# Attention pairs turned by transposing transfers, and the order of the first three pairs

## The chip, the cores and the metric

The kernel runs on one core of a Trainium2 chip. The metric is the device time of one execution in microseconds (us). Five engines work side by side, each through its own list of instructions in order: TensorE (PE, its weight loads PEld), VectorE (DVE), ScalarE (ACT), GpSimd (POOL) and SyncE (SP). SP and ACT also issue transfers (DMA); an instruction that waits holds up everything behind it on its engine.

## What the reference computes

```python
q_n, k_n, c_n = (t / (norm(t, axis=-1) + 1e-6) for t in (q, k, centroids))   # q, k, v: (4, 8, 768, 64)
q_assign = argmax(einsum('bhsd,hcd->bhsc', q_n, c_n), -1)                     # 16 centroids per head
k_assign = argmax(einsum('bhsd,hcd->bhsc', k_n, c_n), -1)
mask = q_assign[:, :, :, None] == k_assign[:, :, None, :]
scores = where(mask, q @ k.T / sqrt(64), -1e9)
x = softmax(scores) @ v            # (4, 8, 768, 64) -> x: (3072, 512)
h = maximum(x @ w_in, 0)           # w_in: 512 x 2048
out = (h * h) @ w_out              # w_out: 2048 x 512
```

A token attends only to tokens of its own cluster, and the result feeds a two-layer network with a squared ReLU.

## The kernel before, in words

The attention goes over 16 pairs of heads (`for p in range(NG)`), the rest of the time is the network. Each engine's order is the order of the program text (a manual schedule), so what stands earlier in the text is issued earlier on that engine.

For each pair the kernel needs `qkT[pair]`, q and k with the head dimension on the partitions, and marks that say which cluster a token belongs to.

- Pair 0 is turned by matmuls against an identity (`turn_first`, L280, copied at L285); pair 1 too, in three parts (`turn`, L295, copied at L299). From pair 2 on, `split_words` copies q and k as 16-bit halves on ACT (L315), stores them to DRAM (`words`, L316), and `turn_words` reads them back with one transposing transfer on SP (L327).
- `logits` (L335) multiplies with the centroids into a bank "ls". `turn_logits` (L346) turns it on DVE and `number` finds the first of the largest logits (L357 to L362). For pair 0 the result is a one-hot tile `oh`, turned by PE in `turn_onehot` (L402). For the other pairs `number` writes small marks (to L379), which go to DRAM and back as `rows`: `far` (L383), then two `rows` transfers (L386) that wait for `far`, all on SP.
- A tile of scores is a mask (L456) and a product (L447) added in a PSUM tile "sc" (`tile_of`), then an exponential on ACT (L463). Nine tiles make a pair. There are three "sc" buffers, used in turn by `begin`: the bank "ls", with the next logits and the sums of `add_up` (L500), takes one of the three as well.
- DVE adds the exponentials up (L466). PE multiplies with v (`times_v`, L481, banks V and M). `add_up` sums over partitions, `invert` (L509, L513) takes reciprocals and stores them (`far_r`, L515), `spread` reads them back into `rb` for all partitions (two transfers, L522), and `finish` (L545) scales a pair's result with `rb`. `finish(p - 1)` stands behind pair p's additions on DVE, followed by `round_2` (L151 to L159) on a block of w_in. At the top of pair p + 1 come `invert(p)`, `turn_logits` and `number` of pair p + 2.
- `load_qk`, `load_v` and `load_ahead` (blocks of weights, L128) issue loads on SP, except that from pair 4 on q and k go through ACT's queue.

Pools: six buffers for q and k ("qk", also used by `flat`), nine for exponentials ("ex"), three `qkT`.

Of the kernel before, what the change touches and what calls it, by code (L numbers as in the profile page):

```python
# [8 lines left out]
F32 = mybir.dt.float32  # L9
# [9 lines left out]
P = 128  # L19
# [6 lines left out]
def kernel(  # L26
# [196 lines left out]

    seen = const.tile([P, NG * NBL], F32, name="seen")

    oh = accp.tile([P, NBL, 2, D], BF16, name="oh", tag="part")
# [10 lines left out]
    def centroids_norm():  # L237
        sq = once.tile([P, D], F32, name="cen_sq")
        ss = const.tile([P, 1], F32, name="cen_ss")
        nc.vector.tensor_tensor(out=sq, in0=cen, in1=cen, op=ALU.mult)  # L240
        nc.vector.reduce_sum(out=ss, in_=sq, axis=AX.X)
        nc.vector.tensor_scalar_max(out=ss, in0=ss, scalar1=1e-30)
        nrm = const.tile([P, 1], F32, name="cen_nrm")
        nc.scalar.sqrt(nrm, ss)
        warm = once.tile([P, 1], F32, name="warm")
        nc.scalar.activation(out=warm, in_=ss, func=ACT.Exp, scale=0.0)
        for _ in range(2):
            r = small.tile([P, 1], F32, name="cen_r")
            nc.vector.reciprocal(out=r, in_=nrm)
            twice = small.tile([P, 1], F32, name="cen_twice")  # L250
            nc.vector.scalar_tensor_tensor(
                out=twice, in0=ss, scalar=r, in1=nrm, op0=ALU.mult, op1=ALU.add
            )
            nc.vector.tensor_scalar_mul(out=nrm, in0=twice, scalar1=0.5)
        nc.vector.tensor_scalar_add(out=nrm, in0=nrm, scalar1=1e-6)
        rden = const.tile([P, 1], F32, name="cen_rden")
        nc.vector.reciprocal(out=rden, in_=nrm)
        for e in range(2):
            nc.vector.tensor_scalar(
                out=cn[:, e], in0=cen, scalar1=rden, scalar2=odd[:, e : e + 1],  # L260
                op0=ALU.mult, op1=ALU.mult,
            )
# [25 lines left out]

    def turn(pair, part, bank):
        if part == 0:  # L290
            qkT[pair] = qktp.tile([P, 2 * NCH, P], F32, name="qkT")
        for i in range(4):
            which, c = divmod(4 * part + i, NCH)
            for e in range(2):
                nc.tensor.matmul(  # L295
                    bank[D * e : D * (e + 1), P * i : P * (i + 1)],
                    lhsT=raw[pair][which][:, e, c], rhs=ident, start=True, stop=True,
                )
        nc.scalar.copy(  # L299
            out=qkT[pair][:, 4 * part : 4 * part + 4].rearrange("p c n -> p (c n)"), in_=bank  # L300
        )
        if part == 2:
            raw.pop(pair)

    words = {}

    def split_words(pair, which, queue=nc.sync):
        if pair >= NG:
            return
        if which == 0:  # L310
            words[pair] = dram.tile([2 * NCH, P, 2, 2 * D], U16, name="words")
        flat = loads.tile([P, NCH, 2, 2 * D], U16, name="flat", tag="qk")
        src = raw[pair][which].bitcast(U16).rearrange("p h c (d two) -> p h c two d", two=2)
# [9 lines left out]
    def turn_words(pair):  # L323
        if pair >= NG:
            return
        qkT[pair] = qktp.tile([P, 2 * NCH, P], F32, name="qkT")
        nc.sync.dma_start(  # L327
            qkT[pair].rearrange("p c n -> p (c n)").bitcast(U16),
            words.pop(pair).rearrange("c p two d -> (c p two) d"), transpose=True,
        )  # L330

# [16 lines left out]
    def number(pair):  # L348
# [7 lines left out]

        nc.vector.reduce_max(out=mx, in_=src, axis=AX.X)  # L357
        nc.vector.tensor_tensor(out=best, in0=src, in1=over_c(mx), op=ALU.is_ge)
        nc.vector.tensor_tensor(
            out=best, in0=best, in1=order.unsqueeze(1).to_broadcast([P, n, C]), op=ALU.mult  # L360
        )
        nc.vector.reduce_max(out=mx, in_=best, axis=AX.X)  # L362
        if pair == 0:
            nc.vector.tensor_tensor(
                out=oh.rearrange("p b e c -> p (b e) c")[:, :, 0:C], in0=best, in1=over_c(mx),
                op=ALU.is_equal,
            )
            return
        squared = small.tile([P, n], F32, name="squared")
# [15 lines left out]
        for e in range(2):  # L385
# [3 lines left out]
            )  # L389

    def turn_onehot():
        spare = expp.tile([P, 2, 512], F32, name="ex").bitcast(BF16)
# [3 lines left out]

        for half, bank in enumerate((sc.pop("oh")[:, 0], M)):
            n = NBL // 2
# [204 lines left out]
    def load_ahead(rounded):  # L603
        nonlocal loaded
        while loaded < min(rounded + (6 if stage_2 else 3), N_IN + FT):
            load_weights(loaded)
            loaded += 1

    centroids_norm()
    turn_first(0, 0, V, nc.scalar.copy)  # L610
# [3 lines left out]
    centroids_turned()  # L614
    turn_first(1, 1, halves[1], nc.vector.tensor_copy)
    logits(0, begin("ls"))
    for i in ("oh", 0, 1):
        begin(i)
    turn_logits(0)
    number(0)  # L620

    first_sums = []
# [7 lines left out]
    for p in range(NG):  # L630
        if p == 0:
            load_qk(3)
            load_ahead(0)
        if p == HP + 1:
            nc.sync.dma_start(x_far[FEED[3]], xT.pop(FEED[3]))
        if p:
            invert(p - 1)
            if p == NG - 1:
                early_x_sums()
            turn_words(p + 2)  # L640
            spread(p - 1)
        if 2 < p + 1 < NG:
            turn_logits(p + 1)
            number(p + 1)
        load_v(p + 1)
        if p:
            load_ahead(p - 1)


        if p == 0:  # L650
            for i in range(2):
                turn(1, i, (V, M)[i])
                score(p, i, 0, True)
            turn_onehot()
            for t in rows_of:
                nc.vector.memset(t, 0.0)
            turn(1, 2, V)
            for i in range(NB):
                if i == 2:
                    begin(i)  # L660
                    score(p, i, 0, True)
                mask(p, i, 0, False)
                exponential(i)
        else:
            for i in range(NB):
                tile_of(p, i)
        total[p] = endp.tile([P, 2, S], F32, name="total")
        first, last = total[p][:, :, 0:QA], total[p][:, :, QA:S]
        add(nc.vector, first, ex[0], ex[1])
        if p == 1:  # L670
            tile_of(p, NB)
        if p < 2:
            logits(p + 1, begin("ls"))
            turn_logits(p + 1)
            number(p + 1)
        add(nc.vector, first, first, ex[2])
        for i in range(NB, NCH):
            if p != 1 or i > NB:
                tile_of(p, i)
            add(nc.vector, first, first, ex[i])  # L680
        if p == 0:
            for i in range(2):
                split_words(2, i, nc.scalar)
            turn_words(2)
        else:
            split_words(p + 3, 0)


        for i in range(NCH, NCH + NB):
            tile_of(p, i)  # L690
        part = accp.tile([P, 2, 512], F32, name="part")
        add(nc.vector, part, ex[NCH], ex[NCH + 1])
# [1011 lines left out]
    def fine_sums():  # L1704
        nc.vector.scalar_tensor_tensor(
            out=seen, in0=seen, scalar=2.0 ** -100, in1=seen, op0=ALU.is_ge, op1=ALU.is_gt,
            accum_out=fine,
        )

    def check_sums():  # L1710
        every = more.tile([1, 1], F32, name="every", tag="more")
        nc.tensor.matmul(every, lhsT=fine, rhs=ups[:, 0:1], start=True, stop=True)
        nc.vector.tensor_scalar(
            out=flag[0:1], in0=every, scalar1=UP * float(P * NG * NBL), scalar2=None, op0=ALU.is_lt
        )
# [279 lines left out]
```

## Time and profile before

| | us |
|---|---|
| median of 3 runs (lowest, highest) | 861.9 (861.75, 864.93) |
| the profiled execution's own time | 864.17 |
| its span, first to last instruction | 862.3 |
| PE busy in the span | 854.2 |
| DVE busy | 740.9 |
| ACT busy | 452.6 |
| POOL busy | 246.6 |

The span is what the views of the trace divide up; the profiled execution's own time is 1.87 us longer. The attention takes roughly the first 320 us of it, some 19 us for each pair once it runs evenly. The first three pairs, the ones that the change touches, lie before 75 us.

### The profile page before, as it was taken

To read this page: it belongs to the slowest core of one execution; us is meant where nothing else is said; L and a number is where in the kernel's file an instruction comes from. 1 tells how busy PE (TensorE), PEld (TensorE's weight loads), DVE (VectorE), ACT (ScalarE), POOL (GpSimd) and SP (SyncE) were. 2 spreads that over 40 slices of the span, in tenths; PEclk is the share of its full clock that TensorE was granted. 3 is DMA by queue.
4 is the path that set the end of the run, shared out by engine and by line. 5 is a ranking of instruction groups with operands and counts; after the bars stand their busy time and mean duration, and the time that the engine had idled before them with its cause. 6 is when DMAs were issued, how large, how long until landed. Compare 5 with 4: busy or idle time off the path is not lost.

```text
span 862.3 us, 15571 instructions
## 1 busy us (share of the span) xinstructions
PE 854.2 (99%) x5883; PEld 648.9 (75%) x5883; DVE 740.9 (86%) x1192; ACT 452.6 (52%) x697; POOL 246.6 (29%) x232
## 2 busy tenths in 40 slices
PE   9999999999999999999999999999999999999997
PEld 6444444444444445557899999999999999999997
DVE  5799888888888899899788988799888997888786
ACT  4877766677776557753212683222268322584120
POOL 0000001000000046772587537130223902337000
PEclk9999999999999999999999999999999999999999
DMA  7676797777766217829897744459447895434542
GB/s 258 156 199 178 202 285 202 192 184 197 196 173 179 67 44 240 259 73 322 326 334 279 235 159 156 175 165 338 145 183 234 289 364 200 181 137 137 219 153 72
DMA packets 149732, 174.36 MB, mean 202 GB/s; under 512 B 57258, under 2 KB 126994, under 8 KB 146322
## 3 DMA queue, kind: packets, MB, share of 16 engines
q1 hardware_dynamic: 133090, 152.94, 56.2%
q10 hardware_dynamic: 16560, 20.35, 7.2%
q8 instruction: 48, 0.79, 0.4%
q14 instruction: 34, 0.28, 0.1%
HBM read 111.98 MB, written 50.27 MB: 188 GB/s over the span
## 4 chain that ended last, share of the span: by engine, by line
PE 92%; DVE 4%; ACT 2%; issue 1%; DMA 0%; DVEq 0%
PE bank L1390 22%; PE bank L1113 17%; PE sc L447 14%; PE av_a L481 10%; PE bank L811 7%; PE bank L1287 6%; PE more L1113 5%; PE av_b L481 5%; PE sc L456 4%; PE sc L335 1%; PE sc L500 1%; DVE home L557 1%; ACT g L786 1%; ACT g L787 1%; DVE w_raw L155 1%
## 5 line engine op out<-in xcount | busy, mean ns | idle before, releaser
L463 ACT ACTIVATE ex<-sc 128x1024 f32<-128x1024 f32 x144 | 144.4, 1026 | 37.5 <-PE sc L447 31.6
L447 PE MATMUL sc<-qkT 64*128 64x512 f32 (+1 forms) x768 | 150.5, 484 | 0.0
L167 POOL TENSOR_TENSOR w_in<-w_in,w_raw 128x512 int32<-128x512 int32 x16 | 21.4, 1335 | 296.4 <-DVE w_in L159 296.4
L1098 POOL TENSOR_TENSOR g<-g,home 128x384 f32<-128x384 f32 x60 | 60.4, 1038 | 155.4 <-DVE home L1202 101.9
L447 PEld LDWEIGHTS sc<-qkT 64*128 64x128 f32 x768 | 65.7, 188 | 42.1 <-issue 30.2
L481 PE MATMUL av_a<-ex,v_raw 128*64 128x512 f32 x384 | 85.9, 596 | 0.0
L466 DVE TENSOR_TENSOR total<-total,ex 128x1024 f32<-128x1024 f32 x64 | 78.7, 1229 | 6.5
L1647 ACT COPY spare<-bank 128x128 f32<-128x128 f32 x35 | 9.2, 263 | 132.3 <-issue 69.7
L1390 PE MATMUL bank<-wt,l 128*128 128x128 f32 x544 | 72.0, 275 | 0.4 <-DVE l L557 0.4
L1390 PE MATMUL bank<-wt,home 128*128 128x128 f32 x552 | 70.5, 275 | 0.0
L1390 PEld LDWEIGHTS bank<-wt,l 128*128 128x128 f32 x544 | 66.2, 192 | 0.6 <-DVE l L557 0.6
L1390 PEld LDWEIGHTS bank<-wt,home 128*128 128x128 f32 x552 | 66.0, 192 | 0.0
L481 PEld LDWEIGHTS av_a<-ex,v_raw 128*64 128x64 f32 x384 | 26.2, 137 | 51.0 <-issue 50.3
L1202 DVE TENSOR_TENSOR g<-bank,g 128x384 f32<-128x384 f32 (+2 forms) x108 | 53.2, 505 | 10.7 <-PE bank L1113 6.6
L1080 ACT COPY home<-bank 128x384 f32<-128x384 f32 x66 | 30.9, 480 | 54.9 <-PE bank L1113 53.5
L456 PE MATMUL sc<-rows 64*128 64x512 bf16 (+1 forms) x360 | 58.8, 323 | 0.0
L786 ACT ACTIVATE g<-g 128x768 f32<-128x768 f32 (+1 forms) x77 | 54.8, 712 | 4.6 <-DVE g L1202 3.3
L787 ACT ACTIVATE g<-g 128x768 f32<-128x768 f32 (+1 forms) x77 | 55.7, 723 | 2.4
L481 PE MATMUL av_b<-ex,v_raw 128*64 128x256 f32 x384 | 44.2, 379 | 0.0
L481 PEld LDWEIGHTS av_b<-ex,v_raw 128*64 128x64 f32 x384 | 27.6, 137 | 20.7 <-issue 5.7
L456 PEld LDWEIGHTS <-rows 64*128 64x128 bf16 x360 | 17.5, 94 | 33.6 <-issue 30.4
L1390 PE MATMUL bank<-wt,g 128*128 128x128 f32 x304 | 39.1, 276 | 0.0
(296 smaller groups left out, 1857.4 us busy)
## 6 DMA issues: line engine op xcount, KB each, us to landing
wt<-right_far SPq DMA_DIRECT2D x11, 1792.0 KB
wt<-w_far SPq DMA_DIRECT2D x20, 896.0 KB
words<-flat SPq DMA_DIRECT2D x26, 384.0 KB
w_raw<-in_moe_w_in_dram SPq DMA_DIRECT2D x16, 512.0 KB
w_raw<-in_moe_w_out_dram SPq DMA_DIRECT2D x16, 512.0 KB
wt<-right_far SPq DMA_DIRECT2D x7, 1024.0 KB
v_raw<-in_v_dram SPq DMA_DIRECT2D x16, 384.0 KB
raw<-raw_far SPq DMA_DIRECT2D x12, 512.0 KB
```

Of the source, the lines that this page charges most:

```text
L447: nc.tensor.matmul(sc[i][:, e, cols], lhsT=qkT[pair][rows, NCH + c], rhs=qkT[pair][rows, n.start // P : n.stop // P], start=first, stop=no ...
L456: nc.tensor.matmul(sc[i][:, e, cols], lhsT=ohT[pair][rows, 1, c * P : (c + 1) * P], rhs=ohT[pair][rows, 0, columns(i)], start=first, stop= ...
L463: nc.scalar.activation(out=ex[i], in_=sc.pop(i), func=ACT.Exp, scale=SCALE)
L466: eng.tensor_tensor(out=out, in0=a, in1=b, op=ALU.add)
L481: nc.tensor.matmul(bank[D * e : D * (e + 1), 0 : n.stop - n.start], lhsT=raw_v[pair][:, e, c], rhs=ex[i][:, e, cols], start=c == 0, stop=c ...
L786: nc.scalar.activation(out=to, in_=to, func=ACT.Relu)
L787: nc.scalar.square(to, to)
L811: nc.tensor.matmul(bank, lhsT=operands[j][0][:, kk], rhs=operands[j][1][:, kk], start=(kk == 0), stop=(kk == H2 - 1),)
L1098: nc.gpsimd.tensor_tensor(out=of_four(to, s)[:, f, half], in0=of_four(base, s)[:, f, half], in1=beside[s][:, u], op=ALU.add,)
L1113: nc.tensor.matmul(bank[:, QT * u : QT * (u + 1)], lhsT=lefts[j, s](u)[i], rhs=operand[i], start=begins and u == 0, stop=True, skip_group_ ...
L1202: nc.vector.tensor_tensor(out=out, in0=one, in1=two, op=ALU.add)
L1390: nc.tensor.matmul(bank, lhsT=left[:, f], rhs=rhs[:, f], start=(f == 0), stop=(f == F4 - 1))
```

## The change

Pair 1 is no longer turned by PE. `split_words(1, ..)` runs on ACT before the loop, with its two `flat` tiles in "ex" buffers, and `turn_words(1)` issues two transposing transfers, one for q and one for k. On SP this stands ahead of `load_qk(3)` and of two blocks of weights (three before). The last copy of pair 0's k is shared by ACT and DVE (`by_two`).

Pair 0's marks are written straight from the comparison with the maximum; `count_marks` counts them into the tile `single`, and the check at the end takes it in.

Pair 0's third score now stands before the masks. `logits(1)`, its turning and numbering move from the fourth tile of pair 0 to behind its eighth, into bank M, followed by `turn_words(2)` and `load_v(1)` on SP. Pair 1 computes two scores before its first mask, which needs `rows`. `logits(2)` and `number(2)` move from behind its fourth tile to behind its sixth, and `spread(0)` and the third block of weights come behind `number(2)`; `load_v(2)` comes ahead of `turn_words(3)`.

```diff
@@ split_words / turn_words
-        flat = loads.tile([P, NCH, 2, 2 * D], U16, name="flat", tag="qk")
+        if pair == 1:
+            spare = expp.tile([P, 2, 512], F32, name="ex").bitcast(U16)
+            flat = spare.rearrange("p a n -> p (a n)")[:, 0 : 4 * S // 2].rearrange(
+                "p (c two d) -> p c two d", c=NCH, two=2
+            )
+        else:
+            flat = loads.tile([P, NCH, 2, 2 * D], U16, name="flat", tag="qk")
...
-        nc.sync.dma_start(
-            qkT[pair].rearrange("p c n -> p (c n)").bitcast(U16),
-            words.pop(pair).rearrange("c p two d -> (c p two) d"), transpose=True,
-        )
+        far = words.pop(pair)
+        for i in range(0, 2 * NCH, NCH if pair == 1 else 2 * NCH):
+            c = slice(i, i + (NCH if pair == 1 else 2 * NCH))
+            nc.sync.dma_start(
+                qkT[pair][:, c].rearrange("p c n -> p (c n)").bitcast(U16),
+                far[c].rearrange("c p two d -> (c p two) d"), transpose=True,
+            )
@@ number
+        if pair == 0:
+            nc.vector.tensor_tensor(
+                out=oh.rearrange("p b e c -> p (b e) c")[:, :, 0:C], in0=src, in1=over_c(mx),
+                op=ALU.is_ge,
+            )
+            return
...
-        if pair == 0:
-            nc.vector.tensor_tensor(
-                out=oh.rearrange("p b e c -> p (b e) c")[:, :, 0:C], in0=best, in1=over_c(mx),
-                op=ALU.is_equal,
-            )
-            return
@@ new functions
+    def count_marks():
+        marked = small.tile([P, 1], F32, name="marked")
+        nc.vector.reduce_sum(
+            out=marked, in_=oh.rearrange("p b e c -> p (b e) c")[:, :, 0:C], axis=AX.XY
+        )
+        nc.vector.tensor_scalar(
+            out=single, in0=marked, scalar1=2.0 * NBL, scalar2=None, op0=ALU.is_equal
+        )
+    def by_two(out, in_):
+        nc.scalar.copy(out=out[:, 0:QT], in_=in_[:, 0:QT])
+        nc.vector.tensor_copy(out=out[:, QT:], in_=in_[:, QT:])
@@ before the loop
-    turn_first(1, 1, halves[1], nc.vector.tensor_copy)
+    turn_first(1, 1, halves[1], by_two)
     logits(0, begin("ls"))
-    for i in ("oh", 0, 1):
+    for i in range(2):
         begin(i)
     turn_logits(0)
     number(0)
+    for i in range(2):
+        split_words(1, i, nc.scalar)
@@ the loop
         if p == 0:
+            turn_words(1)
             load_qk(3)
-            load_ahead(0)
+            load_ahead(-1)
         if p:
             invert(p - 1)
...
+            if p == 1:
+                load_v(2)
             turn_words(p + 2)
-            spread(p - 1)
+            if p > 1:
+                spread(p - 1)
...
-        load_v(p + 1)
-        if p:
+        if p > 1:
+            load_v(p + 1)
             load_ahead(p - 1)
         if p == 0:
             for i in range(2):
-                turn(1, i, (V, M)[i])
                 score(p, i, 0, True)
             turn_onehot()
+            count_marks()
             for t in rows_of:
                 nc.vector.memset(t, 0.0)
-            turn(1, 2, V)
+            begin(2)
+            score(p, 2, 0, True)
             for i in range(NB):
-                if i == 2:
-                    begin(i)
-                    score(p, i, 0, True)
                 mask(p, i, 0, False)
                 exponential(i)
+        elif p == 1:
+            for i in range(2):
+                begin(i)
+                score(p, i, 0, True)
+            for i in range(2):
+                mask(p, i, 0, False)
+                exponential(i)
+            tile_of(p, 2)
...
-        if p == 1:
-            tile_of(p, NB)
-        if p < 2:
-            logits(p + 1, begin("ls"))
-            turn_logits(p + 1)
-            number(p + 1)
         add(nc.vector, first, first, ex[2])
         for i in range(NB, NCH):
-            if p != 1 or i > NB:
-                tile_of(p, i)
-            add(nc.vector, first, first, ex[i])
+            tile_of(p, i)
+            if p == 1 and i + 1 == NCH:
+                logits(2, begin("ls"))
+                turn_logits(2)
+                number(2)
+                spread(0)
+                load_ahead(0)
+            if p or i + 1 < NCH:
+                add(nc.vector, first, first, ex[i])
         if p == 0:
             for i in range(2):
                 split_words(2, i, nc.scalar)
-            turn_words(2)
...
         for i in range(NCH, NCH + NB):
             tile_of(p, i)
+            if p == 0 and i == NCH + 1:
+                sc["ls"] = M.rearrange("p (a n) -> p a n", a=1)
+                logits(1, sc["ls"])
+                turn_logits(1)
+                number(1)
+                turn_words(2)
+                load_v(1)
+                add(nc.vector, first, first, ex[NCH - 1])
@@ fine_sums
+        add(nc.vector, fine, fine, single)
```

## Rows read from the trace of the kernel before

**Rows 1.** The page: busy time of each engine; the chain that ended last.
```profile
PE 854.2 (99%) x5883; PEld 648.9 (75%) x5883; DVE 740.9 (86%) x1192; ACT 452.6 (52%) x697; POOL 246.6 (29%) x232
...
PE 92%; DVE 4%; ACT 2%; issue 1%; DMA 0%; DVEq 0%
```

**Rows 2.** Chain of work in order of time, first 60 us: start, us, what.
```profile
11.79 1.02 PE av_a L295 x16
...
18.39 1.85 ACT ex L463 x2
...
26.95 5.30 PE av_a L481 x24
...
34.84 0.78 PE sc L500 x8
...
36.80 0.22 PE sc L456 x2
37.02 0.86 PE sc L447 x4
```

**Rows 3.** Timeline of all engines, 0 to 45 us; DVE rows: start, us, instruction.
```profile
10.35 0.56 DVE L285 COPY qkT<-sc 128x384 f32<-128x384 f32 x1 [0.79 <-PE sc L280]
...
13.04 0.56 DVE L358 TENSOR_TENSOR best<-lt,mx 128x384 bf16<-128x384 f32 x1
...
14.81 0.56 DVE L364 TENSOR_TENSOR oh<-best,mx 128x384 bf16<-128x384 bf16 x1
...
21.41 0.58 DVE L346 STREAM_TRANSPOSE lt<-sc 128x384 f32<-128x384 f32 x1
...
25.32 0.28 DVE L379 STREAM_TRANSPOSE marks_t<-marks 128x96 bf16<-128x96 bf16 x1
```

**Rows 4.** Timeline of ACT, 9 to 60 us.
```profile
16.44 0.87 ACT L410 ACTIVATE ex<-sc 128x384 bf16<-128x384 bf16 x2 [0.90 <-PE sc L402]
...
18.29 2.86 ACT L463 ACTIVATE ex<-sc 128x1024 f32<-128x1024 f32 x3
...
24.64 1.55 ACT L315 COPY flat<-q_raw 128x768 uint16<-128x768 uint16 x2
26.23 0.41 ACTq L316 DMA_DIRECT2D words<-flat  x1
26.73 1.57 ACT L315 COPY flat<-k_raw 128x768 uint16<-128x768 uint16 x2 [0.53 <-ACT flat L315]
```

**Rows 5.** Timeline of SP, 24 to 75 us: times in which SP issued transfers.
```profile
25.63 0.38 SPq L383 DMA_DIRECT2D far<-marks_t  x1
28.59 1.68 SPq L386 DMA_DIRECT2D rows<-far  x2
31.35 5.36 SPq L327 DMA_TRANSPOSE qkT<-words  x1
...
44.77 1.22 SPq L522 DMA_DIRECT2D rb<-far_r  x2
...
47.67 0.42 SPq L383 DMA_DIRECT2D far<-marks_t  x1
51.24 1.52 SPq L386 DMA_DIRECT2D rows<-far  x2
```

**Rows 6.** Timeline of DVE, 34 to 78 us.
```profile
45.00 5.18 DVE L466 TENSOR_TENSOR total<-total,ex 128x1024 f32<-128x1024 f32 x4
...
53.28 1.61 DVE L545 SCALAR_TENSOR_TENSOR xT<-xT,rb 128x384 f32<-128x384 f32 x2
...
57.09 0.52 DVE L346 STREAM_TRANSPOSE lt<-sc 128x384 f32<-128x384 f32 x1
```

**Rows 7.** Timeline of all engines, 46 to 60 us: third tile of pair 2.
```profile
57.66 0.10 PEld L456 LDWEIGHTS <-rows 64*128 64x128 bf16 x2 [0.60 <-DVE lt L346]
```

**Rows 8.** Windows of the last stretch: busy time of each engine, PEclk, DMA share.
```profile
856.00:858.00 2.00, 1.06 (x10) 0.87 (x8) 1.08 (x3) 0.00 (x0) 0.00 (x0) 1.00 0.14 46
858.00:860.00 2.00, 0.00 (x0) 0.00 (x0) 0.00 (x0) 0.00 (x0) 0.00 (x0) 0.91 0.39 114
860.00:862.30 2.30, 0.00 (x0) 0.00 (x0) 0.00 (x0) 0.00 (x0) 0.00 (x0) 0.50 0.03 11
```

More of the change, by code (lines that the diff above doesn't have):

```diff
@@ L224 @@
     seen = const.tile([P, NG * NBL], F32, name="seen")
+    single = const.tile([P, 1], F32, name="cen_ss")
     oh = accp.tile([P, NBL, 2, D], BF16, name="oh", tag="part")
@@ L238, in centroids_norm @@
         sq = once.tile([P, D], F32, name="cen_sq")
-        ss = const.tile([P, 1], F32, name="cen_ss")
+        ss = single
         nc.vector.tensor_tensor(out=sq, in0=cen, in1=cen, op=ALU.mult)
@@ L287, in turn_first @@
             raw.pop(0)
[L289 to L297, printed above, removed]
-                )
-        nc.scalar.copy(
-            out=qkT[pair][:, 4 * part : 4 * part + 4].rearrange("p c n -> p (c n)"), in_=bank
-        )
-        if part == 2:
-            raw.pop(pair)
     words = {}
@@ L326, in turn_words @@
         qkT[pair] = qktp.tile([P, 2 * NCH, P], F32, name="qkT")
-        nc.sync.dma_start(
-            qkT[pair].rearrange("p c n -> p (c n)").bitcast(U16),
-            words.pop(pair).rearrange("c p two d -> (c p two) d"), transpose=True,
-        )
+        far = words.pop(pair)
[5 more added lines that the diff above has]
+            )
     def logits(pair, bank):
@@ L362, in number @@
         nc.vector.reduce_max(out=mx, in_=best, axis=AX.X)
-        if pair == 0:
-            nc.vector.tensor_tensor(
-                out=oh.rearrange("p b e c -> p (b e) c")[:, :, 0:C], in0=best, in1=over_c(mx),
-                op=ALU.is_equal,
-            )
-            return
         squared = small.tile([P, n], F32, name="squared")
@@ L395, in turn_onehot @@
         )
-        for half, bank in enumerate((sc.pop("oh")[:, 0], M)):
+        for half, bank in enumerate((V, M)):
             n = NBL // 2
@@ L607, in load_ahead @@
             loaded += 1
+    def by_two(out, in_):
+        nc.scalar.copy(out=out[:, 0:QT], in_=in_[:, 0:QT])
+        nc.vector.tensor_copy(out=out[:, QT:], in_=in_[:, QT:])
+    QT = TB // 2
     centroids_norm()
@@ L1713, in check_sums @@
         nc.vector.tensor_scalar(
-            out=flag[0:1], in0=every, scalar1=UP * float(P * NG * NBL), scalar2=None, op0=ALU.is_lt
+            out=flag[0:1], in0=every, scalar1=UP * float(P * (NG * NBL + 1)), scalar2=None, op0=ALU.is_lt
         )
```

## The prediction, made before the changed kernel was run

> **What bounds the kernel now.** I read the page first: PE is busy for 854.2 of 862.3 us, and the chain that ended last is 92% PE [rows 1]. So whatever moves PE's list of instructions moves the end, one for one, and nothing else does. Then I followed the chain in order of time through the first three pairs [rows 2]: PE without a break, except for 1.85 us of exponentials from 18.39. There the reader is to see PE turning pair 1 (a group of 16 instructions at L295, one of three), the products with v from 26.95, and pair 0's sums ending at 35.62. Last I read the timelines of DVE, ACT and SP for what stands just behind PE: what is late next if PE comes early [rows 3 to 7]. The telling one is small: the weight load of pair 2's third tile waited for `lt`, DVE's reading of the bank "ls", which ended at 57.61 [rows 6, 7]. In that place DVE, not PE, already ends last, by a hair.
>
> **The opening, where PE gains.** The three groups at L295 go: 3 x 1.02 = 3.1 us of PE. `number(0)` ends with the comparison that stood at 13.04 and ends at 13.60, in place of one that ends at 15.37: 1.8 us less on DVE. `by_two` halves a copy of 0.56 us [rows 3]; I take 0.2 off. So pair 0's logits end near 11.6 (11.8 before, where the next group begins [rows 2]), two scores at 0.86 to 1.06 bring PE to 13.5, and `oh` is ready at 13.4. Twelve small transposes (0.8) and the third score bring it to 15.2.
>
> Against this stands ACT. Before it may copy the turned marks it now splits pair 1's words: each half took 2.1 us from first copy to next copy, the issue included [rows 4]. From 10.7 that is 14.8; with the 0.87 us of marks it is 15.7, so the first mask waits some 0.5 us and the first exponential starts near 16.2, in place of 18.39: 2.2 us gained.
>
> From there exponentials take 0.95 (2.86 for three [rows 4]) and tiles 1.08 on PE (0.22 + 0.86 [rows 2]). Tile 4 of pair 0 needs the buffer of the first exponential (17.15); five tiles end at 22.6, `logits(1)` (0.78, as before, only later) at 23.4, tile 9 at 24.5. Products with v and sums took 34.84 + 0.78 - 26.95 = 8.67, so pair 0 ends at 33.2 in place of 35.62. The gain here is 2.4 us. `count_marks`, like one reduction and one tiny operation, costs DVE under 1 us; the wait for the second exponential (18.1) hides it, and without that cover it would delay the first addition by as much. One tiny addition at the end of the check is nothing.
>
> **Pair 1's transposing transfers.** They must land by 22.6. The words are issued near 12.3 and 14.4. The second half's store in the trace was issued near 28.3 and SP went on at 31.35, 3.0 us later; both transposes together were 5.36 us of issue [rows 5]. That gives 17.4 for the second half's words, and a half transpose of at most 2.7 us of issue: 20.1, with a landing behind it that the trace does not time. Some 2.5 us are left for it. I cost it at nothing, with 0 to 3 us as bounds. What SP holds back meanwhile (`load_qk(3)`, weights) is needed only near 28 and later.
>
> **Pair 1's marks.** `turn_logits` to the end of the marks is 25.60 - 21.41 = 4.2 [rows 3]. From 23.45 that is 27.7; `far` to `rows` took 2.96 and 3.57 us in two pairs, the `rows` issue 1.6 [rows 5]. So SP is done at 32.3 to 32.9, and a landing of at least 2 us gives 34.3 to 35.5. PE arrives at 33.2 + 2 x 0.86 = 34.9. I take a stall of 0.3: first mask at 35.2, with two scores already done, 2.1 us ahead of before (35.62 + 1.72).
>
> **Where the gain goes.** `spread(0)` now stands on SP behind `number(2)`'s transfers, and DVE's `finish(0)` waits for it. Step by step:
>
> - exponentials from 35.6, the second done at 37.5;
> - four additions at 1.29 (5.18 for four [rows 6]) to 42.7, because `turn_logits(2)` stands behind them on DVE;
> - marks after 4.2, at 46.9. `far` goes out then; before, it went at 47.67;
> - `rows` 3.57 later, at 50.5; `rows` and `rb` issues of 1.52 and 1.22: 53.3 [rows 5]. Before, the `rb` issue began at 44.77 and nothing waited for it;
> - the landing of the second `rb`. No row has it. From below it is nothing, 53.3; `far` needed 2.58 and 3.15 us from the end of its issue (26.01 to 28.59, 48.09 to 51.24 [rows 5]). As `rb` is larger than `far`, I take 2.6: 55.9, with 57.5 as the top (3.15 and another microsecond for a `far` that shares the queues with `load_v`).
>
> DVE itself is at `finish(0)` at 46.9 + 1.3 (one addition left) + 3.1 (50.18 to 53.28 in the trace) = 51.3. It waits 4.6 us. Behind it in DVE's list are `round_2(0)`, `invert(1)` and `turn_logits(3)`, which frees the bank "ls"; from the start of `finish` to the end of `turn_logits` took 57.61 - 53.28 = 4.33 us [rows 6]. So the bank is free at 60.2, and pair 2's third tile, which PE could start at 57.6 - 2.1 = 55.5, starts 60.2 - 57.6 = 2.6 us later than before. From then on PE and DVE stand to each other as they did, and I see nothing that gives the time back.
>
> The Trainium skill bears on this ("DMA: Bandwidth & Descriptors", section "Anatomy of one DMA"): a fixed cost of about 2 us per transfer, mostly the confirmation of the last byte, plus the bytes over 436 GB/s, fitted there on the other descriptor path. The rows show more, 2.58 and 3.15 us behind the issue. By the page's figure both landings together would be about 1.5 us shorter and the change would cost about 1 us instead of 2.6, an estimate from that page.
>
> **Sum.** -2.1 (ahead at pair 1's first mask) + 4.7 (lost at pair 2's third tile) = +2.6 us. Against the profiled execution's own 864.17 (span 862.3 and 1.87 around it) that is 866.8, span 864.9. The median of the runs shown, 861.9, lies 2.3 below that execution, so the forecast for the median is **864.5 us**. Half a per cent, what a measurement of this kernel can tell from no change, is 4.3 us.
>
> **Rivals.**
>
> *The gain stays.* If `rb` lands by 51.3, DVE does not wait and pair 2 runs about 2.1 us ahead: 859.8. The point from which it decides is 53.3, the start of `finish(0)` before: every microsecond earlier is a gain, later a loss. For it: `rb` is wanted by nothing else and the queues may be emptier than in the trace. Against it: even a landing of nothing gives 53.3, so the chain in front would have to be 2 us shorter too. Chance 0.15 for a time between 859 and 861.5.
>
> *The stall lets the clock fall.* PE would idle from 55.5 to 60.2. At the end of the trace PE stops within 856 to 858, and the granted clock is 0.91 in the next window and 0.50 in the last, the level of 1.2 GHz [rows 8]; so a stop of this order can cost the clock. No row has PE working at that level. If tiles 3 to 6 of pair 2 ran at half speed it would be 4 x 1.08 = 4.3 us more: up to 868.8; if the clock holds, or returns at once, nothing. For it: the idle stretch is long. Against it: PE has work on both sides of it, and I cannot place the fall. Chance 0.2, taken at 866 to 869. The Trainium skill says the same ("TensorE: Matmul & The Clock Gate", Part 1): an idle array falls to half its clock and activity gives it back; the trace agrees as to the fall.
>
> *Pair 1's transposes land late.* `logits(1)` then holds PE, and with it the marks, the additions and `rb`: each microsecond late comes on top of the 2.6. With 2 us late, 866.5. For it: a first transposing transfer issued for 5.36 us; against it, 2.5 us of room. Chance 0.1.
>
> **How the numbers follow.** The forecast (0.55) has its own range, 863 to 866: `rb` landing between 54.3 and 57.3. The range for 8 in 10 goes down to 859.8, to hold most of the kept gain, and up to 867.2, to hold the smaller clock losses and late transposes. Slower by over 0.5% (over 866.2): most of the clock case and part of the late transposes, 0.2. Faster by over 0.5% would need 4.3 us, more than PE loses in work: 0.02. Within: 0.78.
>
> **What would show it.** In the changed profile: first exponential near 16.2; pair 0's sums ending near 33.2; `rows` for pair 2 issued near 50.5 and `rb` right behind; DVE idle for some 4 us ahead of L545, released by the `rb` transfer; then PE's third tile of pair 2 waiting for `lt` until about 60. Wrong would be: no idle time of DVE ahead of L545 (then 859.8), PE idle at L335 in pair 0 (late transposes), or a granted clock under 1.00 near 60 us.

## The result, and the profile after

The changed kernel takes 874.39 us (median of 6 runs, 870.92 to 876.72) against 861.83 before (6 runs, 861.13 to 864.93): ratio 1.0128, interval 1.011 to 1.0146. By the medians it is 12.6 us slower, by the ratio 11.0, where 2.6 were forecast. The profiled execution has a span of 874.9 us and a time of 876.72; before, 862.3 and 864.17.

The page of the changed kernel. PE's busy time hardly moved (854.2 before [rows 1], 855.8 now), although the three groups at L295, 3.1 us of work, are gone: some of PE's work ran longer, which the clock will explain, and the rest of what was lost is idle time. In the chain that ended last, PE's share fell from 92% [rows 1] to 82%, and DVE and transfers stand in it instead. PE's list is 48 instructions shorter (5883 before), which will matter below.

```profile
span 874.9 us, 15480 instructions
PE 855.8 (98%) x5835; PEld 649.1 (74%) x5835; DVE 743.0 (85%) x1192; ACT 453.0 (52%) x699; POOL 245.7 (28%) x232
PE 82%; DVE 9%; DMA 4%; ACT 3%; issue 1%; SPq 1%; DVEq 0%; ACTq 0%
```

To see where the idle time lies, I match each PE instruction of the two traces, counted from the last one, and take the difference of their starts, below called the shift. In the changed kernel it is -2.54 us at the end of pair 0, -1.46 at pair 1's products with v, +6.65 at pair 2's third tile, +8.03 behind that tile, +8.75 at 585 us, +13.0 at 617 us and +12.7 at the end. So there are three places: the stall at pair 2 (forecast, too small), the tiles right behind it (a rival) and one at 600 us that I had not seen.

The opening's rows, ACT's first, then PE's: the first exponentials at 15.79 (18.29 before [rows 4]), pair 0's sums from 32.23, pair 1's first mask at 35.13.

```profile
15.79 5.61 ACT L466 ACTIVATE ex<-sc 128x1024 f32<-128x1024 f32 x6 [0.49 <-PE sc L459]
```
```profile
32.23 0.85 PE L503 MATMUL sc<-total,ups 128*32 128x384 f32 x8
...
35.13 1.14 PE L459 MATMUL sc<-rows 64*128 64x512 bf16 x6
```

**The stall at pair 2.** The chain of work of the changed kernel in order of time, 36 to 66 us (start us, us, what):

```profile
38.76 5.43 DMA words<-flat
44.24 3.06 SPq L321
...
47.39 6.50 DMA far<-marks_t
53.91 0.73 SPq L380
...
55.44 0.52 SPq L525
...
56.01 3.92 DMA rb<-far_r
60.03 1.57 DVE xT L548 x2
...
63.88 0.45 DVE lt L340
64.38 0.61 PE sc L459 x2
```

This is the forecast's chain, link by link: `far` of pair 2 (47.39, forecast 46.9), `rows`, `rb`, `finish(0)` at L548, the bank "ls", PE's third tile. Two links are longer than forecast. `far` took 6.50 us where 3.57 was taken from [rows 5], and the second `rb` landed 3.3 us behind the end of its issue (56.74 to 60.03) where 2.6 was taken. The link ahead of them shows what came close to `far`: pair 3's `words` were late, and so SP's transposes for pair 3 went out at 44.24, 3.15 us ahead of `far`; in the kernel before they went out at 41.20, 6.5 us ahead of it:

```profile
41.20 3.51 SPq L327 DMA_TRANSPOSE qkT<-words  x1
```

The timeline of SP shows what stands around `words`: `load_v(1)` ahead of it at 37.63 and `load_v(2)` behind it at 40.71, both moved there by the change. `words` left SP 1.45 us later than before (38.26 against 36.81), and the transposes followed 5.98 us behind instead of 4.39.

```profile
14.76 4.57 SPq L321 DMA_TRANSPOSE qkT<-words  x2
...
37.63 0.57 SPq L105 DMA_DIRECT2D v_raw<-in_v_dram  x1
38.26 1.04 SPq L307 DMA_DIRECT2D words<-flat  x2
39.40 1.22 SPq L518 DMA_DIRECT2D far_r<-seen  x1
40.71 1.06 SPq L105 DMA_DIRECT2D v_raw<-in_v_dram  x1
44.24 3.06 SPq L321 DMA_TRANSPOSE qkT<-words  x1
```

The trace's packets, counted by the microsecond in which they ended, show what lay ahead of `far` (issued at 47.39, its packets are those of 64 bytes; the transposes' have 256; the 1536-byte ones are loads that ACT issued):

```
47  SP's queue: 1053 of 256 B          ACT's queue:  13 of 1536 B
48  SP's queue:  219 of 256 B          ACT's queue: 157 of 1536 B
49  SP's queue:  547 of 256 B          ACT's queue:  61 of 1536 B
50  SP's queue:   75 of 256 B          ACT's queue:  45 of 1536 B
51  SP's queue:    7 of 256 B          ACT's queue: 126 of 1536 B
52  SP's queue:  360 of 64 B           ACT's queue: 109 of 1536 B
```

So a transfer of 24 KB stood some 4 us behind the transposing transfer in front of it. The Trainium skill ("DMA: Bandwidth & Descriptors", section "Queues, rings and completion order") says that each DMA engine takes the descriptors of one queue in their order; the trace agrees, the first packet of 64 bytes ended at 52.39, when the 256-byte ones were over (51.54).

The same rows show a second thing in the way. As ACT's loads came up, the transposes' packets fell from 1053 in a microsecond to 219. These are the loads of pair 5's q and k, in ACT's timeline of the changed kernel:

```profile
45.09 0.38 ACTq L95 DMA_DIRECT2D q_raw<-in_q_dram  x1
45.50 0.48 ACTq L95 DMA_DIRECT2D k_raw<-in_k_dram  x1
```

In the kernel before ACT issued them behind `far` (48.36 and 49.56 against 47.67):

```profile
48.36 0.38 ACTq L95 DMA_DIRECT2D q_raw<-in_q_dram  x1
```

Over all thirteen profiles of this document, `far` of pair 2 took 3.5 to 6.5 us in the seven in which at least one of these loads was issued ahead of it, and 2.9 to 4.0 in the six in which none was. In e6_pad (below) the transposes' last packet ended at 48.62, and `far`'s first began only at 50.51, while ACT's loads ran. No run moves these loads alone, so how the delay of `far` divides between them and the transposes is not shown.

DVE's timeline shows the wait that came of it, 8.57 us where 4.6 was forecast, and the wait of PE behind it, 5.11:

```profile
50.76 0.69 DVE L469 TENSOR_TENSOR total<-part 128x512 f32<-128x512 f32 x1
60.03 1.57 DVE L548 SCALAR_TENSOR_TENSOR xT<-xT,rb 128x384 f32<-128x384 f32 x2 [8.57 <-DMA rb<-far_r]
...
63.80 0.52 DVE L340 STREAM_TRANSPOSE lt<-sc 128x384 f32<-128x384 f32 x1
```

PE's timeline there:

```profile
53.85 0.85 PE L329 MATMUL sc<-qkT,cnT 128*32 128x384 f32 x8 [1.10 <-DMA qkT<-words]
...
56.16 0.39 PE L459 MATMUL sc<-rows 64*128 64x512 bf16 x1 [0.81 <-DMA rows<-far]
56.95 0.39 PE L459 MATMUL sc<-rows 64*128 64x512 bf16 x1 [0.40 <-DMA rows<-far]
...
64.38 0.61 PE L459 MATMUL sc<-rows 64*128 64x512 bf16 x2 [5.11 <-DVE lt L340]
64.78 1.91 PE L450 MATMUL sc<-qkT 64*128 64x512 f32 x4
```

**The clock behind it.** Windows of the changed kernel (us, busy time and instructions of PE, PEld, DVE, ACT, POOL, then the granted clock, DMA share, GB/s):

```profile
62.00:63.00 1.00, 0.00 (x0) 0.00 (x0) 0.93 (x3) 0.00 (x0) 0.00 (x0) 1.00 1.05 326
63.00:64.00 1.00, 0.00 (x0) 0.00 (x0) 0.97 (x4) 0.00 (x0) 0.79 (x1) 0.88 0.70 212
64.00:65.00 1.00, 0.62 (x4) 0.54 (x6) 0.93 (x3) 0.00 (x0) 0.49 (x1) 0.50 0.33 76
66.00:67.00 1.00, 1.00 (x6) 0.42 (x4) 0.89 (x4) 0.26 (x1) 0.00 (x0) 0.50 0.35 82
67.00:68.00 1.00, 1.00 (x8) 0.43 (x6) 0.97 (x5) 0.76 (x1) 0.00 (x0) 0.91 1.06 162
```

PE stopped, the clock went to the level of 1.2 GHz, and the first tiles ran at that level (four products in 1.91 us above, against 1.02 at full clock) until about 67.2. That is 1.4 us more (6.65 to 8.03).

**The place at 600 us.** SP's timeline, and PE's, of the changed kernel in the third batch:

```profile
585.22 1.31 SPq L1806 DMA_DIRECT2D xT<-x_far  x2
591.31 0.81 SPq L995 DMA_DIRECT2D wt<-w_far  x2
594.11 6.83 SPq L1806 DMA_DIRECT2D xT<-x_far  x2
602.02 0.32 SPq L964 DMA_DIRECT2D raw<-raw_far  x1
602.46 0.36 SPq L964 DMA_DIRECT2D home<-raw_far  x1
```
```profile
608.09 0.89 PE L1140 MATMUL bank<-wt,raw 128*128 128x192 f32 x4 [1.58 <-DMA raw<-raw_far]
609.68 1.42 PE L1140 MATMUL bank<-wt,home 128*128 128x192 f32 x4 [0.70 <-DMA home<-raw_far]
```

and SP's timeline of the kernel before at the same place:

```profile
576.47 1.31 SPq L1778 DMA_DIRECT2D xT<-x_far  x2
584.22 0.81 SPq L968 DMA_DIRECT2D wt<-w_far  x2
585.40 0.97 SPq L1778 DMA_DIRECT2D xT<-x_far  x2
589.20 0.32 SPq L937 DMA_DIRECT2D raw<-raw_far  x1
```

The second pair of loads of x takes 6.83 us to issue in place of 0.97, the loads behind it on SP come 4 us later against the rest, and PE, which does not wait here in the kernel before, waits 2.3 us for them. The windows then show the clock again at 0.50 (610 to 612 us) and 0.67 (612 to 614). The diff touches nothing there.

### The profile page after: what moved, and what is told of

It is laid out like the page before. It is cut to its first block, busy times and chain, and to the rows that moved or that the text cites. A ratio compares the mean times of both kernels' runs of the same rounds, so it can differ in the third digit from the quotient of the medians.

```text
span 874.9 us, 15480 instructions
## 1 busy us (share of the span) xinstructions
PE 855.8 (98%) x5835; PEld 649.1 (74%) x5835; DVE 743.0 (85%) x1192; ACT 453.0 (52%) x699; POOL 245.7 (28%) x232
## 4 chain that ended last, share of the span: by engine, by line
PE 82%; DVE 9%; DMA 4%; ACT 3%; issue 1%; SPq 1%; DVEq 0%; ACTq 0%
PE bank L1417 19%; PE bank L1140 16%; PE sc L450 13%; PE av_a L484 8%; PE bank L838 6%; PE more L1140 5%; PE av_b L484 4%; PE bank L1314 4%; PE sc L459 4%; DVE home L560 2%; PE sc L329 1%; DMA far<-marks_t 1%; PE sc L503 1%; DVE g L1229 1%; DMA home<-raw_far 1%
```

## The experiments

Labels stand for kernels made from the changed one, unless it is said otherwise. One correction applies to the shifts of all runs: the start of `logits(0)` varies from run to run (8.09 and 10.03 us in two runs of the changed kernel, 8.60 and 10.23 in two of the kernel before), because the opening products run at half pace for a shorter or longer time; in e9_both_pad and e10_pad_front they also start 1.8 us later, behind the padding. "Loss" is the shift less this difference.

| label | `logits(0)` | loss at pair 2's tile 3 | behind it | 585 us | end | second x loads, us of issue | PE list | ratio (interval) |
|---|---|---|---|---|---|---|---|---|
| changed | 10.03 | 6.9 | 8.2 | 9.0 | 12.9 | 6.83 | 5835 | 1.0128 (1.011-1.0146) |
| e4_after_again | 8.09 | 4.8 | 7.6 | 8.1 | 10.2 | 6.78 | 5835 | one time, 872.27 us |
| e3_v_back | 10.70 | 5.4 | 7.9 | 8.2 | 10.4 | 7.31 | 5835 | 1.0107 (1.0083-1.0131) |
| e1_spread_back | 9.68 | 2.3 | 2.5 | 2.5 | 5.0 | 7.22 | 5835 | 1.0038 (1.002-1.0056) |
| e2_finish_later | 9.99 | 0.0 | 0.1 | 4.0 | 7.1 | 7.38 | 5835 | 1.0073 (1.0053-1.0094) |
| e7_both | 8.77 | 0.2 | 0.3 | 0.6 | 2.6 | 7.03 | 5835 | 1.0041 (1.0021-1.006) |
| e8_before_spread | 7.78 | 5.4 | 5.4 | 5.7 | 5.5 | 0.98 | 5883 | 1.0062 (1.0037-1.0088) |
| e6_pad | 9.05 | 5.6 | 7.1 | 7.0 | 6.7 | 0.97 | 5883 | 1.0075 (1.0047-1.0104) |
| e10_pad_front | 10.71 | 5.0 | 6.7 | 6.6 | 6.3 | 1.00 | 5883 | 1.0101 (1.0081-1.012) |
| e9_both_pad | 10.71 | 0.5 | 0.6 | 2.2 | 2.9 | 0.94 | 5883 | 1.0021 (1.001-1.0032) |
| e11_both_tiny | 9.76 | 2.6 | 2.8 | 3.5 | 3.2 | 0.92 | 5883 | 1.0014 (0.9996-1.0031) |
| e5_before_again | 8.60 | 0 | 0 | 0.8 | 0.6 | 0.98 | 5883 | one time, 863.06 us |

**e1_spread_back** puts pair 0's reciprocals back ahead of pair 2's marks on SP.

```diff
-            if p > 1:
-                spread(p - 1)
+            spread(p - 1)
...
                 number(2)
-                spread(0)
```

> The changed kernel with spread(0) back ahead of number(2) on SP. Theory A (DVE's finish(0) waits for rb, holds the bank ls and with it PE): rb is issued near 47 and lands by 51, DVE does not wait ahead of finish, and the third tile of pair 2 does not wait for lt. What is left is that rows for pair 2 come some 1.2 us later than in the changed kernel, so PE's first mask of pair 2 waits until about 58: near 864, 862 to 866. Theory B (pair 2's marks are late because SP's transfers in front of them are, and the place of spread is of no account): rows later still, PE waits as long as in the changed kernel, 870 or more. Without the later stall near 605 us of the changed profile; with it, 3 to 4.5 us more in either theory.

Ratio 1.0038: the place of `spread(0)` alone carries 0.9% of the 1.28%. DVE waits 1.58 us ahead of L548 and its start is 52.44; PE no longer waits for `lt`. But the kernel is not faster than before either: `rb` (47.18) and `far` (48.44) stand behind pair 3's transposes (44.39), `rows` are issued at 52.56, PE waits 1.8 us for them, and the clock falls after that. Windows of e1_spread_back:

```profile
54.00:56.00 2.00, 0.61 (x3) 0.32 (x5) 1.93 (x5) 0.12 (x1) 0.30 (x1) 0.98 0.50 124
56.00:58.00 2.00, 2.00 (x8) 1.15 (x7) 1.88 (x5) 0.00 (x0) 0.98 (x1) 0.50 0.93 283
```

**e8_before_spread** is the other half of the pair: the kernel before, with nothing but `spread(0)` moved behind pair 2's `number`.

```diff
-            spread(p - 1)
+            if p > 1:
+                spread(p - 1)
...
             number(p + 1)
+            if p == 1:
+                spread(0)
```

> The kernel before with one edit of the change alone: spread(0) behind number(2) on SP. Theory A: rb lands near 55 and not near 48, DVE waits some 2 us ahead of finish(0), and pair 2's third tile comes about 2 us later, with up to 1.7 more for a fall of the clock: 864 to 866 where before has 862. Theory B: nothing but far earlier by 1 us: no change.

Ratio 1.0062, 5.0 us by the medians. Of the loss of 5.4 in the profile, 2.0 arise in pair 1, ahead of the moved step: the opening was early in this run, and PE reached `logits(2)` before its words were turned. The other 3.4 are the stall at pair 2's third tile. So the moved step is harmful by itself, without the edits of the opening, and its price was 3.4 us, DVE's wait of 3.39, where I had forecast a wait of 4.6 for the whole change. The time of the run, 5.0 us above before, is beyond the 2 to 4 that I expected of it. DVE's row, then PE's, of e8_before_spread:

```profile
56.33 1.59 DVE L545 SCALAR_TENSOR_TENSOR xT<-xT,rb 128x384 f32<-128x384 f32 x2 [3.39 <-DMA rb<-far_r]
```
```profile
60.70 0.39 PE L456 MATMUL sc<-rows 64*128 64x512 bf16 x2 [3.21 <-DVE lt L346]
```

Here too the second `rb` landed 3.9 us behind its issue (51.31 + 1.16 to 56.33), and `far` took 4.0 (45.80 to 49.78). And here PE stood still for 3.2 us without a fall of the clock.

**e2_finish_later** leaves `spread(0)` where the change has it, and has DVE read pair 3's logits before it waits for `rb`.

```diff
             turn_words(p + 2)
+            if p == 2:
+                turn_logits(3)
+                finish(0)
+                round_2(0)
+                round_3(0)
...
-        if p:
+        if p > 1:
             finish(p - 1)
```

> The changed kernel with finish(0) and round_2(0) behind turn_logits(3) on DVE; the order on SP is the same. Theory A: the bank ls is free near 56 whatever rb does, PE does not wait for lt, no fall of the clock near 64; PE keeps the wait for rows (pair 2 begins 1.4 us later than before), and DVE, late by some 5 us, holds pair 2's sums for about 1 us: +2.5 against before, 864.4, 862 to 867. Theory B: same as the changed kernel, 870 or more. The later stall near 605 us would add 3 to 4.5.

The loss at the third tile is gone (0.0): the stall of PE ran through the bank "ls". DVE's timeline of e2_finish_later shows the wait in its new place, harmless for the bank:

```profile
54.73 0.52 DVE L340 STREAM_TRANSPOSE lt<-sc 128x384 f32<-128x384 f32 x1
58.26 1.60 DVE L548 SCALAR_TENSOR_TENSOR xT<-xT,rb 128x384 f32<-128x384 f32 x2 [3.01 <-DMA rb<-far_r]
```

It is harmful elsewhere: DVE has pair 2's work 3 us later, PE waits for it between 74 and 80 us (0.68 us for `total`, 1.13 for `lt`), and 2.9 us are lost by 100 us, 4.0 by 585. The wait was only moved on a busy engine, and it came back.

**e3_v_back** undoes the other move: v of pair 1 early again, v of pair 2 behind `spread(0)`.

```diff
             load_ahead(-1)
+            load_v(1)
...
-            if p == 1:
-                load_v(2)
...
                 spread(0)
+                load_v(2)
...
-                load_v(1)
                 add(nc.vector, first, first, ex[NCH - 1])
```

> The changed kernel with load_v(1) back ahead of pair 0 and load_v(2) behind spread(0) on SP. The words of pair 3 are then issued near 37.7 and land near 41, the transposes go at 41 to 44 and are through by 46, so far for pair 2 takes about 3 us and not 6.5. Theory A as first forecast: rb lands near 56, DVE still waits 4 us, the third tile of pair 2 is 2.6 us later than before, perhaps with a fall of the clock (1.4): 864.5 to 866. Theory B: with the transfers in front of the marks on time the whole loss goes: 860.

`far` of pair 2 now takes 3.5 us (49.29 to 52.76), as forecast from [rows 5], and DVE's wait shrinks from 8.57 to 5.65. But the early load costs as much elsewhere: measured from `logits(0)`, pair 1's `rows` are issued 1.15 us later than in the changed kernel (33.10 and 10.70 against 31.28 and 10.03), and PE is 1.4 us further behind by 38 us. Loss 5.4 in place of 6.9, between the 6.9 and the 4.8 that the changed kernel itself shows in two profiles, and the total hardly differs: 873.47 us, neither of the two times that I expected.

Nor did `far` become short in the way that I expected. Pair 3's transposes were to go out at 41 to 44 and went out at 44.95, measured from `logits(0)` no earlier than in the changed kernel (34.25 and 34.21 behind it). What differs is what is near `far`: it went out 4.3 us behind the transposes instead of 3.15, their packets took 3.2 us (46.19 to 49.39) instead of 6.05 (45.49 to 51.54), and ACT's loads came later, at 47.11. So the run shows that `far` is short again when the loads of v stand elsewhere; by which way is open.

**e4_after_again** and **e5_before_again** are the two kernels unchanged, to see how much one kernel varies between executions.

> The changed kernel unchanged, for a second profile. If the stall of PE near 605 us (2.3 us idle and a fall of the clock behind it) belongs to the change, it is there again and the shift against before grows from about 8.5 at 585 us to about 13 at 617. If it is chance of the transfers in that one execution, the shift stays near 8 and the span is near 870.

> The kernel before, unchanged, for a second profile. The five profiles of the changed kernel and its variants all have PE waiting for raw near the start of the third batch (599 to 609 us), the profile of before has not, though both programs are the same there. If that belongs to the program (theory C: where an engine's instructions are fetched, which fell near 580.5 in before and some 2.7 us later, counted from the work around it, in the others), this profile again has no wait there and a packet of the instruction queue near 580. If it is chance of one execution, it may have the wait.

The stall's loss of the same program was 6.9 in one execution and 4.8 in the other (`far` of pair 2 took 6.5 and 5.3 us), and the clock stayed low for 3.4 us (63.8 to 67.2) in the one and for some 6.8 in the other, so that behind it the two are 8.2 and 7.6: where the stall is shorter the clock took more. The place at 600 us is in both runs of the changed kernel and in neither of the kernel before.

**e6_pad** adds 24 tiny products (48 instructions) in front of pair 2's third tile; they write to a bank that is overwritten.

```diff
             for i in range(NB):
+                if p == 2 and i == 2:
+                    for _ in range(24):
+                        nc.tensor.matmul(
+                            V[0:32, 0:4], lhsT=ident[:, 0:32], rhs=ident[:, 0:4],
+                            start=True, stop=True,
+                        )
                 tile_of(p, i)
```

> The changed kernel with 24 tiny f32 matmuls into the unused bank V, ahead of pair 2's third tile, where PE is idle for 5 us; their result is not used. The program then has as many PE instructions in front of the third batch as the kernel before. Theory C: the instruction packet moves back to the place it had, PE does not wait for raw, and the shift against before stays what it was at 585 us: some 3 us less than the changed kernel, near 870; less still if the tiny matmuls keep the clock up. If the wait belongs to something else (transfers issued, addresses), it stays, 873 to 875.

PE's timeline and a window of e6_pad:

```profile
57.11 1.68 PE L688 MATMUL av_a<-ident 128*32 128x4 f32 x48
62.11 0.61 PE L459 MATMUL sc<-rows 64*128 64x512 bf16 x2 [3.32 <-DVE lt L340]
```
```profile
62.00:64.00 2.00, 1.89 (x6) 0.80 (x8) 1.86 (x5) 0.00 (x0) 0.23 (x1) 0.50 0.31 55
```

The stall and the clock's fall stayed. What went is the place at 600 us: PE's list is again 5883 long, the second x loads are issued in 0.97 us, and nothing is lost behind 585 us. So the two losses are separate.

**e7_both** takes both moves out: `spread(0)` back, v of pair 1 on ACT's queue, v of pair 2 behind the marks.

```diff
-    def load_v(pair):
+    def load_v(pair, queue=nc.sync):
...
-            if p == 1:
-                load_v(2)
             turn_words(p + 2)
-            if p > 1:
-                spread(p - 1)
+            spread(p - 1)
...
+            load_v(1, nc.scalar)
             tile_of(p, 2)
...
                 number(2)
-                spread(0)
+                load_v(2)
...
-                load_v(1)
```

> The changed kernel with spread(0) back ahead of number(2), load_v(1) on ACT's queue behind pair 1's second exponential and load_v(2) behind number(2). Theory A together with the late transfers in front of the marks: words of pair 3 land near 41, transposes go at 41 to 44, rb by 48, far for pair 2 at 46.5 takes 3 us, rows land by 53, and pair 2 begins ahead of before by some 2 us with no idle time and no fall of the clock: 860, or 863 with the later wait for raw. If the words and far are no earlier for it, 866 to 868 as e1_spread_back.

Loss 0.2 at pair 2: no wait of DVE ahead of L548 (51.37), `far` 2.9 us (47.18 to 50.04), no fall of the clock. By its shift alone (-1.3) it seemed to keep the opening's gain; measured from `logits(0)` it keeps none. The 2.3 us won in pair 0 go in pair 1, where PE waits 1.3 us for `rows` and 0.7 for an exponential. Then 2 us are lost at 600 us. Ratio 1.0041.

**e10_pad_front** and **e9_both_pad** put the 24 tiny products ahead of the warm-up products, into the changed kernel and into e7_both; **e11_both_tiny** has 30 tiny ones in place of the warm-up.

```diff
+    for _ in range(24):
+        nc.tensor.matmul(
+            warm_up[0:32, 0, 0:4], lhsT=zeros[:, 0:32], rhs=zeros[:, 0:4], start=True, stop=True
+        )
     for _ in range(6):
         nc.tensor.matmul(warm_up[:, 0, 0:P], lhsT=zeros, rhs=zeros, start=True, stop=True)
```

> The changed kernel with the same 24 tiny products ahead of the warm-up, in place of pair 2 as in e6_pad. Theory: the stall at pair 2's third tile and its clock loss stay (6 to 8 us behind by 70 us, as in the changed kernel), and the wait for raw near 600 us and what the clock lost there (2.5 to 4.6 us) go: 868.5 to 870.5, ratio about 1.008. Rival (the later wait hangs on PE's time, or e6_pad lost it by where its products stood): the wait stays and the time is that of the changed kernel, about 873 to 874.

> e7_both with 24 tiny float32 products (32 columns by 4) added ahead of the six warm-up products, while PE waits for the first loads anyway. Their result is overwritten; nothing else of the computation changes. They bring PE's list back to the length it has in the kernel before. Theory: e7_both's gain of 1.5 us was lost near 600 us only because the packet of the instruction queue, whose place hangs on the length of PE's list, fell later among the loads of x. Then PE does not wait for raw near 600 us, and the kernel stands 1 to 1.5 us ahead of the kernel before to the end: ratio 0.998 to 0.9995. Rival: the wait for raw comes of PE being at another time against SP's loads; then it stays, and the ratio is that of e7_both, 1.004.

> As e9_both_pad, but all 30 warm-up products are tiny ones (the six large ones are replaced), because in e9_both_pad the six large ones then ended at 6.6 and logits of pair 0 began at 10.71 where the changed kernel begins them at 10.03. Nothing that reaches the output changes. Theory: the opening gain of 1.2 to 1.6 us of e7_both is kept, no wait for raw near 600 us: span 860.5 to 861.5, ratio 0.998 to 0.9995. Rivals: the turning of pair 0 runs at the low clock for longer without the large products, and the opening gain falls below 1 us (ratio 1.000); or rows for pairs 2 and 3 come later than PE as in e9_both_pad, 1 to 2.5 us (ratio 1.001 to 1.003).

In all three the place at 600 us is mended, wherever the padding stands; SP's timeline of e9_both_pad:

```profile
588.12 0.94 SPq L1807 DMA_DIRECT2D xT<-x_far  x2
591.88 0.32 SPq L965 DMA_DIRECT2D raw<-raw_far  x1
```

With e10_pad_front the loss stays at 6.3 to 6.7 behind the stall, against 12.9 at the end of the changed kernel. By the ratios it is 0.27% faster than the changed kernel, with intervals that overlap, and less fast than expected (1.0101 for 1.008), so the size of that term rests on the profiles; the interval of e6_pad does lie below that of the changed kernel. The best of the versions are e9_both_pad and e11_both_tiny; neither beats the kernel before. My expectation for them (0.998 to 0.9995) was missed; it rested on the gain that I had misread in e7_both. e11_both_tiny shows once more what is left: two waits for pair 2's `rows`, together 1.9 us, and the clock at 0.50 from 57 to 60 us.

## Why the prediction was wrong

**The opening: right.** First exponential 15.79 (forecast 16.2), pair 0's sums end at 33.1 (32.23 + 0.85; forecast 33.2), gain 2.54 (2.4). Of each, 0.2 is this run's earlier start of `logits(0)` and not `by_two`, behind which `logits(0)` took 1.71 us where it had taken 1.57. Pair 1's transposes cost nothing, as forecast: they were issued from 14.76 in 4.57 us, and `logits(1)` did not wait. Pair 1's first mask came at 35.13 (35.2), released by `rows`. For the edits taken at nothing these times leave no visible cost.

**Where the gain goes: the mechanism right, the size wrong.** Each link of the chain came true: marks at 47.16 (46.9), DVE at `finish(0)` at 51.45 (51.3), DVE idle ahead of `finish(0)`, 4.3 us from there to the free bank (4.33), the third tile right behind. The start of `finish(0)` was 60.03 where 55.9 was forecast. The 4.1 us between are three terms: `far` went out 0.5 later; it took 6.5 and not 3.57 (+2.95), the step "`rows` 3.57 later, at 50.5"; and `rb` landed 3.3 behind its issue and not 2.6 (+0.7), 3.9 in e8_before_spread. The second is the step that failed: I took the duration of `far` from a place where only a load of v stood just in front of it on SP's queue and the transposes 6.5 us ahead, and did not ask what would stand there after the change. There it was the transposes, 3.15 us ahead, and ACT's loads of pair 5's q and k. I had costed company only as "another microsecond" at the top of one range. The size varies: in the second profile of the changed kernel `far` took 5.3 us, and the moved loads of v bring it back to 3.5 in e3_v_back and, with `spread(0)` back as well, to 2.9 in e7_both. Which of the two neighbours costs how much is open.

The length of PE's stop, 5.11 us where 4.7 were forecast, is near by luck: both of its ends came 4 us late. PE reached the third tile at 59.27 and not at 55.5, because it had waited 1.10 us for pair 3's turned words and 0.81 and 0.40 for pair 2's `rows`, for which the forecast had nothing. Behind the stall these waits cost nothing more; in e1_spread_back and e11_both_tiny, without the stall, such waits are what is left.

**The rival of the clock came true on top, not instead.** It was priced at up to 4.3 us from four tiles at half pace and given 0.2, against a stop of 4.7 us. The stop was 5.11 us (4.55 in e4_after_again); it cost 1.4 and 2.8 us. All five profiles in which PE stopped for 3 us or more at the third tile with the early opening (the changed kernel twice, e3_v_back, e6_pad, e10_pad_front) have the fall. The chance should have been the larger part.

**The step that I had not written: 600 us.** "From then on PE and DVE stand to each other as they did, and I see nothing that gives the time back" is false for SP's loads. What the runs show: the second pair of x loads takes 6.8 to 7.4 us to issue in all six profiles with 5835 PE instructions, and 0.92 to 1.00 in all seven with 5883, the kernel before included. It follows the length of PE's list, not PE's time: e10_pad_front issues these loads at 592.47 and does it in 1.00, e7_both at 584.44 and takes 7.03. The loss between 585 us and the end is 2.0 to 4 us in the one group and -0.3 to 0.7 in the other. The waits of SP's queue name what it waits for, transfers of ACT (`out_dram<-g`, 6.1 us for one of them); in the kernel before a wait of that kind, 6.4 us, stands ahead of the loads of `wt` instead. Why the list's length matters is only argued: a packet of 16 KB on the queue that the page calls "instruction" falls at 580.5 us before. Set against the shift, one falls within 0.1 us of that place in the six other profiles with 5883 instructions, and 2.6 to 2.7 us later in all six with 5835. That the order in which the loads and stores land turns with this packet is a guess that fits; no run moves the packet alone.

With these terms the median lies above all that the prediction priced; its highest rival, the clock's, ended at 869. In sum, for the profiled execution (+12.6): gain in the opening -1.5 as it stood at the products with v, stall +8.1, clock +1.4, drift to 585 us +0.7, 600 us +3.9.

What remains open: why the opening's gain survives in none of the versions. In e7_both it goes mostly to `rows` of pair 1, in e9_both_pad to a wait of 1.1 us for an exponential in pair 1 and to `rows` of pair 2 (0.8 us, and 1.1 more for `rows` at 134 us), in e11_both_tiny to `rows` of pair 2. So the chain from marks to `rows` looks like the next bound, but no version with a shorter chain was run.

## What to carry to other kernels

When a transfer is moved on a queue, price every later transfer of that queue by what will then stand in front of it, not by its duration in the old trace: the same 24 KB, pair 2's `far`, took 2.9 to 4.0 us in six profiles and up to 6.5 where a transposing transfer and another engine's loads ran close ahead of it. A chain of small transfers (marks, `far`, `rows`) that follows the engine's work by a fixed time eats the gain of an earlier start, so look for it before counting one. And compare profiles from an event behind the opening, and read the place where a loss arises, before tying it to an edit: here a fifth to a third of it arose 500 us behind the last edited step.

## What the runs showed of the hardware

The clock did not follow the length of PE's stop alone: it fell after waits of 0.70 and 1.22 us for `rows` in e11_both_tiny, and not in a stop of 3.21 us in e8_before_spread. It stayed at 0.50 for 3.4 to 6.8 us, most of which PE worked. The Trainium skill ("TensorE: Matmul & The Clock Gate", Part 1) has the array at half its clock when idle and at the full one after activity; the traces agree as to both directions. The opening's products ran at two paces with the granted clock shown as 1.00: twelve of them, on the same inputs, took 1.54 us in the kernel before (from 4.72) and 0.88 in e8_before_spread (from 4.60), and `logits(0)` came 2.45 us earlier there.
